# Dealing the last quarter of an MLP output product between the steps of the next product's first quarter

## The chip, the cores and the metric

The kernel runs on one core of one Trainium2 chip. The metric is the device time of one execution in microseconds (us). Most executions of one kernel agree closely. Five engines run side by side, each with its own instruction queue that is worked off in order: TensorE (PE: matrix products, and PEld: its weight loads), VectorE (DVE), ScalarE (ACT), GpSimd (POOL) and SyncE (SP), which here only issues DMA transfers. POOL issues transfers too, the indirect ones (rows picked by an index list) among them.

## The reference, cut to what matters

The reference is one transformer block, forward and backward: `out`, and the gradients of all inputs and weights, for 2048 tokens of width 1024 and an MLP width of 3584, in bf16. The part that counts here is the MLP.

```
x1  = x + ga * fft_filter(LN(x)*(1+ca)+sa)          # earlier in the kernel
n3  = LN(LN(x1)*(1+cb)+sb)
z   = n3 @ w1 + b1 ;  h = gelu(z)                   # "z" blocks
out = x1 + gb * (h @ w2 + b2)                       # output product, "bo"
gz  = (grad_out*gb) @ w2.T * gelu'(z)               # kept in HBM as d_gz
gn3 = gz @ w1.T                                     # input-gradient product, "pg"
... layer-norm backward of gn3, column sums, then the weight gradients
```

## The kernel before, in words

The tokens are cut into four quarters (blocks b = 0 to 3) of 512. The output product of a quarter (`bo_pass`, L802) runs in two passes, h = 0 and 1, one for each half of the width. A pass has seven steps; a step loads 512 KB of `w2` (L812) and issues 16 matmuls of 128x512 into four PSUM banks (L817). Before the first step, four small matmuls put the bias into the banks (L808). After the seventh, ScalarE copies the banks into the tile `otile` (L826), VectorE makes three products and sums of it (L173, the helper `tt`), and the result goes to `out_0` in three transfers: a direct one issued by SP (L155) and then two indirect ones issued by POOL (L160), which in the program wait one for the other. One late part, four matmuls `pa` (L836), sums the columns of a product for the gradient of `gb`; it is taken up a little later by the generator's second `next`.

A list, `plan`, written out by hand, sets the order of z blocks and output steps. In the last quarter (b = 3) no z block is left, so its 14 output steps follow each other. I call them B1 to B14 (B1 to B7 are h = 0, B8 to B14 are h = 1). `ordered()` chains each matmul of these parts behind the last, so TensorE keeps the written order; all other instructions are placed by a scheduler, which also sets the order in the DMA queues.

Then comes the input-gradient product. It needs `w1` transposed: seven tiles `w1T` are loaded with transposing transfers (L949), into buffers that the z blocks' `w1` tiles leave. For each quarter, seven 512 KB tiles of `gz` are loaded (L989, tiles `gzr` in the buffers t0 to t3), and two passes of seven steps of 16 matmuls fill four PSUM banks each (L996). I call the 14 steps of the first quarter G1 to G14. ScalarE copies the banks out with row sums (L1001, tiles `gn3a` and `gn3b` by turns). VectorE then works through a layer-norm backward (L895 to L900, the tile `got` takes its products), a product `pru`, a second layer-norm backward (L1017 and L895 to L900), and `au`. TensorE sums the columns of `gn3`, `pru` and `au` into `acc3a` and `acc3b` (L193), in 24 matmuls a quarter, placed among the next quarter's `pg` matmuls. `got` lies in the buffer that `otile` had, so nothing is written there before the last transfer out of `otile` has landed. Beside this chain, `gmod_ring` (L916 on) makes eight steps for row 5 of the `w_mod` gradient (L934, L936, tiles `gmw` and `gmg`), which need the finished column sum of `gb`, that is the last `pa`, through `d_gmod` in HBM.

Of the kernel before, what the change touches and what calls it, by code (L numbers as in the profile page):

```python
# [10 lines left out]
FP32 = mybir.dt.float32  # L11
BF16 = mybir.dt.bfloat16
I32 = mybir.dt.int32
ACT = mybir.ActivationFunctionType
# [3 lines left out]
P = 128  # L18
S = 2048
D = 1024  # L20
# [4 lines left out]
KH = D // 2  # L25
# [5 lines left out]
NB = 4  # L31
BW = S // NB
# [3 lines left out]
def kernel(  # L36
# [24 lines left out]
    nc = tc.nc  # L61
# [3 lines left out]
    small = ctx.enter_context(tc.tile_pool(name="small", bufs=2))  # L65
    reg = ctx.enter_context(tc.tile_pool(name="reg", bufs=1))
# [4 lines left out]
    W1T = PXT[2:6] + ["sma", "smb", "px0"]  # L71
# [7 lines left out]
    def ps_f(name):  # L79
        return psum.tile([P, 512], FP32, tag="f", name=name, bufs=4)  # L80
# [37 lines left out]
    d_gz_v = d_gz.rearrange("(fc p) s -> p fc s", p=P)  # L118

    def chunk_rows(dt, i):  # L120
        return dt[4 * i * P:4 * (i + 1) * P, :].rearrange("(q p) d -> p q d", p=P)
# [47 lines left out]
    def bcn(row, n):  # L169
        return bass.AP(tensor=row.tensor, offset=row.offset, ap=[row.ap[0], [0, n], row.ap[1]])  # L170

    def tt(out, a, b, op):
        return nc.vector.tensor_tensor(out=out, in0=a, in1=b, op=op)  # L173
# [101 lines left out]
    wt = reg.tile([P, 2, NDC, 256], BF16, name="wt", tag="wt")  # L275
# [44 lines left out]
    for j in range(4):  # L320
        for cch in range(NDC):
# [7 lines left out]
            else:  # L329
                with tc.high_priority():  # L330
                    nc.scalar.activation(out=gBoT[j][:, cch, :], in_=pt[:], func=ACT.Identity, scale=gb_col[:, cch:cch + 1],
                                         accum_out=gu[:, j, cch:cch + 1])
# [315 lines left out]
    last_pe = [None]  # L648

    def ordered():  # L650
        return tc.issue_after(last_pe[0].ins)
# [77 lines left out]
    for g in range(7):  # L729
        wtile = reg.tile([P, NDC, BW], BF16, name=f"w1_{g}", tag=W1T[g])  # L730
# [71 lines left out]

    def bo_pass(b, h):
        cs_ = slice(h * KH, (h + 1) * KH)
        pbs = [(ps_f if b < NB - 1 or h == 0 else (ps_s, ps_d)[k % 2])("pbo") for k in range(4)]
        for i in range(4):
            with ordered():
                last_pe[0] = nc.tensor.matmul(pbs[i][:], lhsT=ones_bf[0:1, :], rhs=b2_row[0:1, cs_], start=True, stop=False)  # L808
        for g in range(7):
            wp = w2p[w2n[0] % 4]  # L810
            w2n[0] += 1
            nc.sync.dma_start(out=wp, in_=w2_v[:, g * 4:(g + 1) * 4, cs_])  # L812
            hh = hh_slots[(b * 7 + g) % 11]
            for i in range(4):
                for k in range(4):
                    with ordered():
                        last_pe[0] = nc.tensor.matmul(pbs[i][:], lhsT=hh[:, k, i * P:(i + 1) * P], rhs=wp[:, k, :],  # L817
                                                      start=False, stop=(g == 6 and k == 3))
            if g < 6:
                yield  # L820
        bo, x1t, go = (otile[0][:, k] for k in range(3))
        nc.sync.dma_start(out=x1t, in_=chunk_rows(d_x1, b)[:, :, cs_])
        load_tok_half(go, grad_out, b, h)
        for i in range(4):
            with tc.high_priority():
                last_ev[0] = nc.scalar.copy(out=bo[:, i, :], in_=pbs[i][:])  # L826
        tt(go, go, bo, ALU.mult)
        tt(bo, bo, bcn(gb_row[:, cs_], 4), ALU.mult)
        tt(bo, bo, x1t, ALU.add)
        store_tok_half(out_0, bo, b, h)  # L830

        yield
        pa = (ps_d if b < NB - 1 else ps_f)("pa")
        for i in range(4):
            with ordered():
                last_pe[0] = nc.tensor.matmul(pa[:], lhsT=ones_bf[:], rhs=go[:, i, :], start=(i == 0), stop=(i == 3))  # L836
        with tc.high_priority():
            if b == 0:
                nc.vector.tensor_copy(out=gacc[:, cs_], in_=pa[0:1, :])  # L839
            else:  # L840
                tt(gacc[:, cs_], gacc[:, cs_], pa[0:1, :], ALU.add)

    def bo_both(b):
        for h in range(2):
            late = bo_pass(b, h)
            for _ in range(7):
                next(late)
                yield
            bo_late.append(late)

    bo_late = []
# [2 lines left out]
    Z_AT = [{1: ((0, 4),), 2: ((0, 5),), 3: ((0, 6),), 4: ((1, 0),), 6: ((1, 1),), 7: ((1, 2),), 9: ((1, 3),), 10: ((1, 4),),  # L854
             11: ((1, 5),), 12: ((1, 6),)}]
    Z_AT += [{k: ((b, g),) for g, k in enumerate((0, 2, 4, 7, 9, 11, 12))} for b in (2, 3)] + [{}]
    for b in range(NB):
        for k in range(14):
            plan += [("z",) + bg for bg in Z_AT[b].get(k, ())] + [("b", b, k)]
    boq = {}  # L860
    for kind, b, g in plan:
# [7 lines left out]
        else:  # L869
# [6 lines left out]
                bo_late.clear()  # L876
            if g == 13:
                next(boq[b], None)
    for late in bo_late:
        next(late, None)  # L880
    store_gmod([gacc[:, 0:KH], gacc[:, KH:D]], 5)

    gb1 = small.tile([P, NFC], FP32, tag="gb1", bufs=1)
# [57 lines left out]
                load_w(n + 2)  # L941
            yield

    w1Ts = []
    for g in range(7):
        wtile = reg.tile([P, 4, D], BF16, name=f"w1T_{g}", tag=W1T[g])
        for k in range(4):
            fc = g * 4 + k
            nc.sync.dma_start_transpose(out=wtile[:, k, :], in_=B_w1[:, fc * P:(fc + 1) * P])  # L949
        w1Ts.append(wtile)  # L950
    gzr = [reg.tile([P, 2, 4, BW], BF16, name=f"gzr{k}", tag=f"t{k}") for k in range(4)]
    gn3s = [reg.tile([P, 4, D], BF16, name="gn3a", tag="uv0"), reg.tile([P, 4, D], BF16, name="gn3b", tag="wt")]
    n3u = reg.tile([P, 4, D], BF16, name="n3u", tag="uv1")
    n2u = reg.tile([P, 4, D], BF16, name="n2u", tag="uv2")
    pru = reg.tile([P, 4, D], BF16, name="pru", tag="uv3")[:]
    got = reg.tile([P, 6, D], BF16, name="got", tag="ot")
    fbuf2 = reg.tile([P, 4, 4, D], BF16, name="fbuf2", tag="fr")
    acc3 = [ps_d("acc3a"), ps_d("acc3b")]
    gzn = 0
    gmw = reg.tile([P, 2, D], BF16, name="gmw", tag="ph")  # L960
    gmg = reg.tile([P, 2, D], BF16, name="gmg", tag="sb")
    early = gmod_ring((5,), [gmw[:, 0], gmw[:, 1], gmg[:, 0]], gmg[:, 1, :])
# [13 lines left out]

    for b in range(NB):
        gn3 = gn3s[b % 2]
        sums = small.tile([P, 2, 4], FP32, tag="sums")
        gzt = []  # L980
        nc.sync.dma_start(out=n3u[:], in_=chunk_rows(d_n3, b))
        nc.sync.dma_start(out=n2u[:], in_=chunk_rows(d_x1, b))
        norm_act(n2u, n2u, 1, b)
        go4 = got[:, 0:4, :]
        load_tok(go4, grad_out, b)
        for g in range(7):
            sl = gzr[gzn % 8 // 2][:, gzn % 2]
            gzn += 1
            nc.sync.dma_start(out=sl, in_=d_gz_v[:, g * 4:(g + 1) * 4, b * BW:(b + 1) * BW])  # L989
            gzt.append(sl)  # L990
        for h in range(2):
            pgs = [ps_f("pg") for _ in range(4)]
            for g in range(7):
                for i in range(4):
                    for k in range(4):
                        nc.tensor.matmul(pgs[i][:], lhsT=gzt[g][:, k, i * P:(i + 1) * P],  # L996
                                         rhs=w1Ts[g][:, k, h * KH:(h + 1) * KH],
                                         start=(g == 0 and k == 0), stop=(g == 6 and k == 3))
            for i in range(4):
                with tc.high_priority():  # L1000
                    nc.scalar.activation(out=gn3[:, i, h * KH:(h + 1) * KH], in_=pgs[i][:], func=ACT.Identity,  # L1001
                                         accum_out=sums[:, h, i:i + 1])
        tt(sums[:, 0, :], sums[:, 0, :], sums[:, 1, :], ALU.add)
        for i in range(4):
            t = 4 * b + i
            ln_bwd(gn3[:, i, :], sums[:, 0, i:i + 1], n3u[:, i, :], stats[:, 2, 0, t:t + 1], gn3[:, i, :], got[:, 4 + i % 2, :])
        next(early, None)
        tt(pru, gn3[:], n2u[:], ALU.mult)
        g2, ftmp = gn3, pru
        if b < NB - 1:  # L1010
            sums3(b, gn3, pru)
        else:
            g2, ftmp = gn3s[0], gzr[0].rearrange("p a b (c d) -> p (a b c d)", c=1).rearrange("p (q d) -> p q d", d=D)
        s2c = small.tile([P, 4], FP32, tag="s2c")
        for i in range(4):
            t = 4 * b + i
            nc.vector.tensor_tensor_reduce(out=g2[:, i, :], in0=gn3[:, i, :], in1=opcb_row, scale=1.0, scalar=0.0,  # L1017
                                           op0=ALU.mult, op1=ALU.add, accum_out=s2c[:, i:i + 1])
            ln_bwd(g2[:, i, :], s2c[:, i:i + 1], n2u[:, i, :], stats[:, 1, 0, t:t + 1], g2[:, i, :], got[:, 4 + i % 2, :])
        next(early, None)  # L1020
        tt(g2[:], g2[:], go4, ALU.add)
        nc.gpsimd.dma_start(out=chunk_rows(d_gx1, b), in_=g2[:])
        nc.sync.dma_start(out=au[:], in_=chunk_rows(d_A, b))
        tt(n3u[:], g2[:], bcn(ga_row, 4), ALU.mult)
        fold_tok(n3u, ftmp)
        fold2_in[b] = fold_d(fbuf2[:, b], n3u[:], ftmp)
        tt(au[:], g2[:], au[:], ALU.mult)
        if b < NB - 1:
            sums3_ga(b, au)
            next(early, None)  # L1030
# [226 lines left out]
```

## Time and profile before

| what | us |
|---|---|
| median of 3 runs | 1522.13 |
| the runs | 1520.72, 1522.13, 1531.21 |
| span of the profiled execution, first to last instruction (the page gives no other time of its own for it) | 1521.4 |
| TensorE busy | 1437.8 |
| VectorE busy | 1072.0 |
| ScalarE busy | 722.1 |
| last quarter of the output product on TensorE | 715.9 to 773.9 |
| first quarter of the input-gradient product starts | 779.8 |
| last matmul of the input-gradient product starts | 996.6 |

All times of single instructions below are counted from the start of the span. In a row of the timeline the first number is the start, the second the busy time of the merged row (so several instructions, where the row ends in x16), then engine, line, operation, tile written <- tiles read; in brackets stands how long the engine was idle before it and what ended that idle time.

### The profile page before, as it was taken

To read this page: it belongs to the slowest core of one execution; us is meant where nothing else is said; L and a number is where in the kernel's file an instruction comes from. 1 tells how busy PE (TensorE), PEld (TensorE's weight loads), DVE (VectorE), ACT (ScalarE), POOL (GpSimd) and SP (SyncE) were. 2 spreads that over 40 slices of the span, in tenths; PEclk is the share of its full clock that TensorE was granted. 3 is DMA by queue.
4 is the path that set the end of the run, shared out by engine and by line. 5 is a ranking of instruction groups with operands and counts; after the bars stand their busy time and mean duration, and the time that the engine had idled before them with its cause. 6 is when DMAs were issued, how large, how long until landed. Compare 5 with 4: busy or idle time off the path is not lost.

```text
span 1521.4 us, 18355 instructions
## 1 busy us (share of the span) xinstructions
PE 1437.8 (95%) x6831; PEld 667.6 (44%) x6831; DVE 1072.0 (70%) x1577; ACT 722.1 (47%) x956; POOL 363.5 (24%) x428
## 2 busy tenths in 40 slices
PE   5889899999999999999989999979998899999998
PEld 2434445444444444444334444434444444444443
DVE  5992868897799887877224977967066666898633
ACT  4765556668876666655012333322522344443211
POOL 5720621111112122220210101311033421322423
PEclk8999999999999999999999999989999999999999
DMA  9972745989587876999956336496288986766996
GB/s 327 282 207 66 198 150 176 280 258 339 193 265 238 211 254 216 257 282 271 322 170 205 135 101 221 109 275 176 63 201 225 235 242 183 197 174 163 257 206 195
DMA packets 358160, 324.27 MB, mean 213 GB/s; under 512 B 209187, under 2 KB 300849, under 8 KB 357816
## 3 DMA queue, kind: packets, MB, share of 16 engines
q1 hardware_dynamic: 324184, 207.71, 52.4%
q0 software_dynamic: 33888, 115.41, 22.5%
q8 instruction: 53, 0.87, 0.2%
q14 instruction: 35, 0.29, 0.1%
HBM read 164.15 MB, written 109.10 MB: 180 GB/s over the span
## 4 chain that ended last, share of the span: by engine, by line
PE 47%; DVE 22%; DMA 10%; issue 10%; ACT 6%; POOL 3%; SPq 1%; POOLq 0%; ACTq 0%; DVEq 0%
PE pbo L817 11%; PE pz L776 9%; PE gw2acc L1090 8%; PE pg L996 5%; DVE ct L173 4%; PE pv L544 3%; PE pu L451 3%; PE gw1acc L1157 2%; PE pp L659 2%; DVE got L895 2%; DVE fbuf L173 1%; DMA gB<-in_grad_out_dram 1%; DVE gn3a L900 1%; DMA out_dram<-otl 1%; DVE gt L173 1%
## 5 line engine op out<-in xcount | busy, mean ns | idle before, releaser
L659 PE MATMUL pp<-gBoT,wt 128*128 128x512 bf16 x896 | 200.4, 379 | 1.9 <-ACT pho L669 1.0
L1157 PE MATMUL gw1acc<-gzh,n3n 128*128 128x512 bf16 x896 | 197.0, 380 | 0.3 <-DMA gzh<-d_gz 0.3
L996 PE MATMUL pg<-w1T,gzr 128*128 128x512 bf16 x896 | 196.3, 380 | 0.4
L776 PEld LDWEIGHTS <-w 128*128 128x128 bf16 x896 | 87.7, 98 | 109.0 <-issue 3.8
L996 PEld LDWEIGHTS <-gzr 128*128 128x128 bf16 x896 | 88.0, 98 | 107.5 <-issue 2.9
L1157 PEld LDWEIGHTS <-n3n 128*128 128x128 bf16 x896 | 87.8, 98 | 104.3 <-issue 0.6
L659 PEld LDWEIGHTS <-wt 128*128 128x128 bf16 x896 | 87.4, 98 | 103.0 <-DMA wt<-in_B_w_dram 1.4
L776 PE MATMUL pz<-n3Tb,w 128*128 128x512 bf16 x448 | 99.1, 379 | 1.5 <-DVE w2sD L839 1.5
L1090 PE MATMUL gw2acc<-gB,hhsA 128*128 128x512 bf16 x448 | 100.1, 379 | 0.0
L776 PE MATMUL pz<-n3Ta,w 128*128 128x512 bf16 x448 | 98.7, 379 | 1.3 <-ACT gt L779 1.3
L817 PEld LDWEIGHTS <-hhA 128*128 128x128 bf16 x608 | 59.9, 99 | 79.0 <-issue 10.8
L1095 ACT CAST gwo<-gw2acc 128x512 bf16<-128x512 f32 x54 | 30.6, 584 | 122.4 <-PE gw2acc L1090 80.1
L779 ACT ACTIVATE gt<-pz,b_col 128x512 bf16<-128x512 f32 x112 | 72.9, 684 | 29.5 <-PE pz L776 29.0
L785 ACT ACTIVATE gt<-gt 128x2048 bf16<-128x2048 bf16 x28 | 53.4, 1910 | 64.4 <-DVE gt L173 64.4
L173 DVE TENSOR_TENSOR gt<-gt,gt 128x2048 bf16<-128x2048 bf16 x56 | 68.5, 1224 | 15.9 <-ACT gt L787 15.1
L1161 ACT CAST gwo<-gw1acc 128x512 bf16<-128x512 f32 x48 | 27.7, 584 | 109.1 <-PE gw1acc L1157 87.5
L173 DVE TENSOR_TENSOR ct<-ct 128x2048 bf16<-128x2048 bf16 x64 | 76.0, 1219 | 0.8
L1090 PE MATMUL gw2acc<-gB,hht 128*128 128x512 bf16 x256 | 58.9, 392 | 8.7 <-DVE gB L173 8.4
L1090 PEld LDWEIGHTS <-hhsA 128*128 128x128 bf16 x448 | 43.8, 98 | 50.4
L781 ACT ACTIVATE gt<-gt 128x2048 bf16<-128x2048 bf16 x28 | 53.5, 1910 | 7.6 <-DVE gb_acc L796 6.9
L787 ACT ACTIVATE gt<-gt 128x2048 bf16<-128x2048 bf16 x28 | 53.3, 1909 | 0.4
L1162 POOL DMA_DIRECT2D out_dram<-gwo x56 | 30.7, 551 | 77.9 <-ACT gwo L1161 38.3
(314 smaller groups left out, 2552.9 us busy)
## 6 DMA issues: line engine op xcount, KB each, us to landing
gzr<-d_gz SPq DMA_DIRECT2D x28, 512.0 KB, 7.7
wblk<-in_w_mod_dram SPq DMA_DIRECT2D x12, 1024.0 KB, 13.4
d_ph<-pho POOLq DMA_DIRECT2D x21, 512.0 KB, 5.2
out_dram<-otl POOLq DMA_DIRECT2D x40, 256.0 KB, 3.7
d_hh<-hhA POOLq DMA_DIRECT2D x19, 512.0 KB, 4.8
w2sD<-in_B_w_dram SPq DMA_DIRECT2D x14, 512.0 KB, 6.1
hhC<-d_ph SPq DMA_DIRECT2D x14, 512.0 KB, 5.1
w2sA<-d_ph SPq DMA_DIRECT2D x14, 512.0 KB, 4.0
```

What stands on the lines that cost most here:

```text
L173: return nc.vector.tensor_tensor(out=out, in0=a, in1=b, op=op)
L451: last_pu[0] = nc.tensor.matmul(pu[:], lhsT=fb[:, i, cl, c8 * P:(c8 + 1) * P], rhs=sm[:, i, :], start=(i == 0), stop=(i == 3))
L659: last_pe[0] = nc.tensor.matmul(pp[:], lhsT=wt[:, fg % 2, cch, k * P:(k + 1) * P], rhs=gBoT[j][:, cch, :], start=(cch == 0), stop=(cch == ...
L776: last_pe[0] = nc.tensor.matmul(pz[:], lhsT=w1s[g][:, cch, k * P:(k + 1) * P], rhs=n3T[:, cch, :], start=(cch == 0), stop=(cch == NDC - 1))
L779: nc.scalar.activation(out=zb[:, k, :], in_=pz[:], func=ACT.Identity, bias=b1_col[:, fc:fc + 1], scale=1.0)
L781: nc.scalar.activation(out=av, in_=zb, func=ACT.Square)
L785: nc.scalar.activation(out=sg, in_=bv, func=ACT.Sigmoid, scale=2.0 * GK)
L787: nc.scalar.activation(out=bv, in_=bv, func=ACT.Sigmoid, scale=-2.0 * GK)
L817: last_pe[0] = nc.tensor.matmul(pbs[i][:], lhsT=hh[:, k, i * P:(i + 1) * P], rhs=wp[:, k, :], start=False, stop=(g == 6 and k == 3))
L996: nc.tensor.matmul(pgs[i][:], lhsT=gzt[g][:, k, i * P:(i + 1) * P], rhs=w1Ts[g][:, k, h * KH:(h + 1) * KH], start=(g == 0 and k == 0), sto ...
L1090: nc.tensor.matmul(acc[:], lhsT=hh_s[hh_o[fc]][:, t, :], rhs=gBs[t // 4][:, t % 4, h * KH:(h + 1) * KH], start=(t == 0), stop=(t == NT - 1))
L1157: nc.tensor.matmul(acc[:], lhsT=n3ns[t // 4][:, t % 4, cch * P:(cch + 1) * P], rhs=gz2[t // 8][:, t % 8, :], start=(t == 0), stop=(t == NT ...
```

## The change

The last quarter leaves `plan`. Its 14 steps are dealt out with the 14 steps of the first input-gradient quarter by a string, in which B is a step of the output product, G one of the input-gradient product and L takes up the late column sums. The `pg` loop becomes a generator `pg_pass`, used with `ordered()` for the first quarter. The `w1T` and `gz` tiles 0 to 2 are asked for ahead of the string, tiles 3 to 6 one by one in the first G steps. The second pass of the last quarter now uses the same four PSUM banks as the first (tag f), the first input-gradient quarter the four banks of tags s and d, and the column sum of the pass B1 to B7 a bank of tag d. `gn3a` moves to the buffer uv3 and `pru` to uv0.

```
-        pbs = [(ps_f if b < NB - 1 or h == 0 else (ps_s, ps_d)[k % 2])("pbo") for k in range(4)]
+        pbs = [ps_f("pbo") for _ in range(4)]
...
-        pa = (ps_d if b < NB - 1 else ps_f)("pa")
+        pa = (ps_d if b < NB - 1 or h == 0 else ps_f)("pa")
...
-    for b in range(NB):
+    for b in range(NB - 1):
         for k in range(14):
             plan += [("z",) + bg for bg in Z_AT[b].get(k, ())] + [("b", b, k)]
...
+    gn3s = [reg.tile([P, 4, D], BF16, name="gn3a", tag="uv3")]
...
+    def pg_pass(b, h, pool):
+        gn3 = gn3s[b % 2]
+        pgs = [pool(k)("pg") for k in range(4)]
+        for g in range(7):
+            for i in range(4):
+                for k in range(4):
+                    with ordered() if b == 0 else ExitStack():
+                        mm = nc.tensor.matmul(pgs[i][:], lhsT=gzs[b, g][:, k, i * P:(i + 1) * P],
+                                              rhs=w1Ts[g][:, k, h * KH:(h + 1) * KH],
+                                              start=(g == 0 and k == 0), stop=(g == 6 and k == 3))
+                    if b == 0:
+                        last_pe[0] = mm
+            if g < 6:
+                yield
+        for i in range(4):
+            with tc.high_priority():
+                nc.scalar.activation(out=gn3[:, i, h * KH:(h + 1) * KH], in_=pgs[i][:], func=ACT.Identity,
+                                     accum_out=g_sums[b][:, h, i:i + 1])
+        yield
+
+    def pg_first():
+        g_sums[0] = small.tile([P, 2, 4], FP32, name="sums", tag="sums")
+        for h in range(2):
+            for g, _ in enumerate(pg_pass(0, h, lambda k: (ps_s, ps_d)[k // 2])):
+                if h == 0 and g + 3 < 7:
+                    load_w1T(g + 3)
+                    load_gz(0, g + 3)
+                yield
+
+    for g in range(3):
+        load_w1T(g)
+        load_gz(0, g)
+    last_bo, pg0 = bo_both(NB - 1), pg_first()
...
+    for step in "BBLBGBGBGBGBGBGBGLBGBGBGBGBGGGL":
+        if step == "L":
+            run_late()
+        else:
+            next(last_bo if step == "B" else pg0)
+    next(last_bo, None)
+    run_late()
     store_gmod([gacc[:, 0:KH], gacc[:, KH:D]], 5)
...
-    pru = reg.tile([P, 4, D], BF16, name="pru", tag="uv3")[:]
+    pru = reg.tile([P, 4, D], BF16, name="pru", tag="uv0")[:]
```

So TensorE's order becomes B1 B2 (late sum of b = 2) B3 G1 B4 G2 B5 G3 B6 G4 B7 G5 B8 G6 B9 G7 (late sum of B1 to B7) B10 G8 B11 G9 B12 G10 B13 G11 B14 G12 G13 G14 (late sum of B8 to B14), and then the second quarter of `pg`.

More of the change, by code (lines that the diff above doesn't have):

```diff
@@ L878, with load_w1T @@
                 next(boq[b], None)
-    for late in bo_late:
-        next(late, None)
+    w1Ts = []
+    gzr = [reg.tile([P, 2, 4, BW], BF16, name=f"gzr{k}", tag=f"t{k}") for k in range(4)]
+    gzs = {}
+    gn3s = [reg.tile([P, 4, D], BF16, name="gn3a", tag="uv3")]
+    g_sums = {}
+    def load_w1T(g):
+        wtile = reg.tile([P, 4, D], BF16, name=f"w1T_{g}", tag=W1T[g])
+        for k in range(4):
+            fc = g * 4 + k
+            nc.sync.dma_start_transpose(out=wtile[:, k, :], in_=B_w1[:, fc * P:(fc + 1) * P])
+        w1Ts.append(wtile)
@@ new lines, in load_gz @@
+    def load_gz(b, g):
+        n = b * 7 + g
+        gzs[b, g] = gzr[n % 8 // 2][:, n % 2]
+        nc.sync.dma_start(out=gzs[b, g], in_=d_gz_v[:, g * 4:(g + 1) * 4, b * BW:(b + 1) * BW])
+    def pg_pass(b, h, pool):
[3 more added lines that the diff above has]
+            for i in range(4):
+                for k in range(4):
+                    with ordered() if b == 0 else ExitStack():
[11 more added lines that the diff above has]
+        yield
@@ new lines, in pg_first, with run_late @@
+    def pg_first():
[10 more added lines that the diff above has]
+    last_bo, pg0 = bo_both(NB - 1), pg_first()
+    def run_late():
+        for late in bo_late:
+            next(late, None)
+        bo_late.clear()
@@ L942, in gmod_ring @@
             yield
[L944 to L952, printed above, removed]
+    gn3s.append(reg.tile([P, 4, D], BF16, name="gn3b", tag="wt"))
     n3u = reg.tile([P, 4, D], BF16, name="n3u", tag="uv1")
     n2u = reg.tile([P, 4, D], BF16, name="n2u", tag="uv2")
-    pru = reg.tile([P, 4, D], BF16, name="pru", tag="uv3")[:]
+    pru = reg.tile([P, 4, D], BF16, name="pru", tag="uv0")[:]
     got = reg.tile([P, 6, D], BF16, name="got", tag="ot")
@@ L958 @@
     acc3 = [ps_d("acc3a"), ps_d("acc3b")]
-    gzn = 0
     gmw = reg.tile([P, 2, D], BF16, name="gmw", tag="ph")
@@ L978 @@
         gn3 = gn3s[b % 2]
-        sums = small.tile([P, 2, 4], FP32, tag="sums")
-        gzt = []
+        if b > 0:
+            g_sums[b] = small.tile([P, 2, 4], FP32, name="sums", tag="sums")
+        sums = g_sums[b]
         nc.sync.dma_start(out=n3u[:], in_=chunk_rows(d_n3, b))
@@ L985 @@
         load_tok(go4, grad_out, b)
[L986 to L992, printed above, removed]
-            for g in range(7):
[L994 to L1002, printed above, removed]
+        if b > 0:
+            for g in range(7):
+                load_gz(b, g)
+            for h in range(2):
+                for _ in pg_pass(b, h, lambda k: ps_f):
+                    pass
         tt(sums[:, 0, :], sums[:, 0, :], sums[:, 1, :], ALU.add)
```

## The prediction

> **What bounds the kernel now.** I read the page first, then TensorE's timeline around the place of the change, then what the waits there hang on, queue by queue.
>
> The page: TensorE is busy for 95% of the span. Only its gaps, and times when it is slow, can be won.
>
> ```profile
> PE 1437.8 (95%) x6831; PEld 667.6 (44%) x6831; DVE 1072.0 (70%) x1577; ACT 722.1 (47%) x956; POOL 363.5 (24%) x428
> ```
>
> TensorE's timeline, from B1 to the first column sums:
>
> ```profile
> 715.11 0.86 PE L808 MATMUL pbo<-b_row,ones_bf 1*128 1x512 bf16 x2 [1.86 <-ACT otile L826]
> 715.90 5.31 PE L817 MATMUL pbo<-w2sD,hhA 128*128 128x512 bf16 x16
> 721.05 3.62 PE L817 MATMUL pbo<-w2sB,hhB 128*128 128x512 bf16 x16
> ...
> 733.23 3.61 PE L817 MATMUL pbo<-w2sD,hhA 128*128 128x512 bf16 x16 [0.67 <-DMA w2sD<-in_B_w_dram]
> ...
> 740.69 3.61 PE L817 MATMUL pbo<-w2sA,hhA 128*128 128x512 bf16 x16 [0.40 <-DMA w2sA<-in_B_w_dram]
> ...
> 747.19 5.30 PE L817 MATMUL pbo<-w2sC,hhA 128*128 128x512 bf16 x16 [1.92 <-DMA w2sC<-in_B_w_dram]
> ...
> 774.32 0.23 PE L188 MATMUL ptr<-fin,gb_bf 128*28 128x128 bf16 x1 [0.24 <-ACT otile L826]
> 778.16 1.86 PE L836 MATMUL pa<-otile,ones_bf 128*128 128x512 bf16 x4 [3.62 <-DVE otile L173]
> 779.83 53.01 PE L996 MATMUL pg<-w1T,gzr 128*128 128x512 bf16 x241
> ```
>
> Two things are to be seen. After B2 the waits are 0.67, 0.40, 1.92, 0.24 and 3.62 us, 6.85 in all. And sixteen matmuls take 3.62 us (3.45 from one group's start to the next, 0.2157 a matmul), but 5.31 and 5.30 right after waits of 1.86 and 1.92 us: a restart costs 1.68 us. After 0.67 it costs nothing. After 3.62 us the late sum takes 1.86 instead of 1.03, and the 241 matmuls 53.01 instead of 52.16 (241 x 0.2157, and 0.16 for the end of the last one): 1.68 again.
>
> Why the `w2` loads are late: the share of the DMA engines in the stretches.
>
> ```profile
> 735.00:748.00 13.00, 10.68 (x48) 4.52 (x47) 0.00 (x0) 1.97 (x4) 3.49 (x4) 0.98 1.08 366
> 800.00:830.00 30.00, 30.00 (x141) 13.61 (x139) 10.65 (x22) 5.50 (x16) 2.69 (x5) 1.00 0.70 227
> ```
>
> The last two columns are DMA share and GB/s: saturated at 735 to 748, not at 800 to 830.
>
> Last, what follows the late output. SP's and POOL's timelines show the store of the last half quarter and the first transfer into its buffer, VectorE's the chain that writes there too:
>
> ```profile
> 725.92 1.28 SPq L155 DMA_DIRECT2D out_dram<-otile  x1
> ...
> 781.95 0.40 SPq L155 DMA_DIRECT2D out_dram<-otile  x1
> ...
> 794.30 0.38 SPq L128 DMA_DIRECT2D got<-in_grad_out_dram  x1
> ```
>
> ```profile
> 785.13 1.00 POOL L160 DMA_INDIRECT out_dram<-otile,xu  x1 [17.33 <-DMA out_dram<-otile]
> 791.15 1.53 POOL L160 DMA_INDIRECT out_dram<-otile,xu  x1 [5.02 <-DMA out_dram<-otile,xu]
> ```
>
> ```profile
> 827.33 1.23 DVE L895 CUSTOM_DVE_ANT_0 got<-gn3a,n3u 128x1024 bf16<-128x1024 bf16 x1 [11.76 <-ACT gn3a L1001]
> ```
>
> From the store's issue to the moment `got` may be written: 794.30 - 781.95 = 12.35 us. Now this is hidden, because VectorE's first write to `got` comes at 827.33. In the changed program that instruction still waits for the same three transfers.
>
> **The change, part by part.** All sums are against the profiled execution (span 1521.4). The median of the runs lies 0.7 above that span, so I add the difference to the median, 1522.1.
>
> *Dealing B and G out.* B3 starts at 725.49, as before: TensorE's order up to there is unchanged. From B3 to B14 lie 12 B and 11 G steps, 368 matmuls, 79.4 us; with the bias (0.86) and a late sum (0.86) B14 ends at 806.6. The `w2` loads have 6.9 us a step instead of 3.45, so the waits of 0.67, 0.40 and 1.92 go, with one restart. The last late sum has G12 to G14 (10.35 us) ahead of it, more than the 5.5 us that ScalarE and VectorE need before it: the 3.62, the 0.24 and the second restart go. Saved: 6.85 + 2 x 1.68 = 10.2.
>
> *Banks.* B8's bias must wait for the copies out of B7's banks; G5 (3.45 us) lies between, and the last copy takes 0.59: nothing; without that cover 1.9, as at 715.11. The late sum behind G7 takes a bank that `pg` has just filled: its copy out is 0.8 us long and starts 0.9 before G7's end, so about 0.4 (bounds 0 and 1.86, that first row). B14 ends at 807.0, G14 at 817.4, the late sum at 818.2, and the second quarter starts at 818.5. Before, the first quarter's 224 matmuls ended at 779.83 + 0.85 + 48.3 = 829.0. TensorE is 10.5 ahead here.
>
> *Loads.* The transposes stand at the same places in SP's queue as before but for the last two (2 x 2.1 us), which go behind the `w2` loads of B3 and B4. Four `gz` loads instead of one go ahead of those. Two transposes less, 3 x 512 KB more at 366 GB/s (4.3 us): the sum is about nothing for B3's load; bounds: nothing, and 4.3 plus a restart, 6.0. Near nothing, since the later `w2` loads gain room. `n3u` and `n2u` go in at about 786, 30 us before use; `gz` tiles of the second quarter follow G8 to G14. Moving `gn3a` and `pru` costs nothing: both buffers are left by then.
>
> *The output's tail, now on VectorE's path.* B14 ends at 807.0, its last copy at 807.8, three VectorE operations of 1.23 later SP stores, at 811.7. With the 12.35 us of the rows above, `got` is free at 824.0. Until then the waiting VectorE instruction holds the whole layer-norm chain of the first quarter behind it, although `gn3a` is there from 818. The other end is the loaded case: from the store at 725.92 to ScalarE's next write into that buffer, at 747.20, it took 21.3 us. I take 12.35, since the DMA engines are not saturated in this stretch.
>
> *The chain after it, by its offsets before.* From the first write to `got` the trace has 5.7 us to the first column sum of `gn3` (833.03), 15.4 to `pru` (842.76) and 39.0 to `au` (866.37).
> - TensorE does 29 `pg` matmuls (6.3 us) and stands at 824.8; the sum is ready at 829.7: a new wait of 4.9 with a restart of 1.68. Two sums and 42 matmuls: 840.9; `pru` is there (839.5). 14 sums, 101 matmuls: 865.7.
> - Row 5 of the `w_mod` gradient, now at 789 to 816 in idle VectorE time, needs the last late sum and moves into this chain: eight steps of 1.15 and 0.44, 12.7 us. Four fall before `au`, 6.4 us, of which some 3 fill the chain's own pauses (1.12, 1.07 and 1.37 before the L900 rows): `au` at 824.0 + 42.5 = 866.5, wait 0.8, sums done at 868.2.
> - Fold work (9.6) and three more such steps (4.8) follow: VectorE starts the second quarter at 881.0 instead of 883.26, although TensorE has finished it at 879.5.
> - TensorE: 78 matmuls to 885.0, wait to 886.7; 40 and `pru` at 896.5, sums to 899.5; 91 to 919.1, `au` at 920.5, done at 922.2. Before that was 924.03, with 11 matmuls less done (605 and 594 by the program order): 1.8 + 2.4 = 4.2 ahead. The third quarter's chain then starts at TensorE's pace, 4.1 ahead, and the rest of the program is ordered as before.
>
> Sum: 10.5 ahead at 818.5; 4.9 + 1.7 and smaller waits lost; 4.1 left. 1522.1 - 4.1 = 1518.0.
>
> [...] The rows show a slow restart after waits of 1.86 and 1.92 us. [...] The granted clock of 0.83 in the stretch 712 to 722, with that 1.86 in it, speaks for the rows. [...]
>
> **The rivals.**
> - *The tail stays hidden.* If the stores land by 819 (7 us), the 4.9 and the restart vanish and all 10.5 stay: 1511.6. For it: the issue-to-landing median of `otile` transfers is 4.6. Against: POOL's two indirect stores follow each other 6.02 us apart. Chance 0.17.
> - *Slower: the tail is as slow as under load.* With 21.3 us `got` is free at 833.0; the whole chain of the first two quarters shifts by 9.0, and 4.2 ahead become 4.8 behind: 1526.9. It decides from 16.5 us on. For it: the three `gz` loads of 512 KB close by. Against: 0.70 DMA share at 800 to 830. Chance 0.15.
> - *The `w2` load of B3 is late* behind four `gz` loads: up to 6.0, 1524.0. Chance 0.08.
> - *Half of the change does not take place*: the transposes keep their places. True by the program order, and without a price.
>
> **How the numbers follow.** The forecast, 1518.0, has 0.55, with an own range of 1514 to 1522 (the tail between 10 and 16 us). The range 1510 to 1528 takes in the rivals at 1511.6, 1524.0 and 1526.9 and leaves out 0.05 of unforeseen cases. A measurement of this kernel tells about 1% (15.2 us) from no change. No case reaches that: even all of the 10.2 us is too little for faster, and slower needs a tail of 33 us or waits that I have not seen. From the unforeseen cases: faster by over 1% 0.05, within 0.89, slower 0.06.
>
> **What would show it.** In the changed profile: no DMA wait before a `pbo` row after B3; the last L836 row without idle time; the first `pg` matmul of the second quarter near 818.5; the first VectorE row that writes `got` near 824, its idle time ended by an `out` transfer and not by `gn3a`; a TensorE wait of some 5 us before the first L193 row; `gmw` rows among those of the first quarter's chain; the last `pg` matmul near 992.5. Wrong would be the forecast if `got` starts before 820 or after 828, if B3 to B7 wait for DMA, or if TensorE makes good the wait of 4.9 later.

## The result and the profile after

The changed kernel takes 1532.03 us (median of 18 runs, 1527.93 to 1539.23); the kernel before, on the same chips, 1525.2 us (median of 18, 1517.02 to 1533.04). The ratio is 1.0053, with a 95% interval from 1.0038 to 1.0068: some 8 us slower (1525.2 x 0.0053 = 8.1), where 4.1 us less was forecast. The profiled execution of the changed kernel has a span of 1537.1 us and a time of its own of 1539.23, the longest of its 18, so some of its waits can be longer than usual; the experiments show that the one before B3 is.

First the page's line of busy times. TensorE's work is the same (some of its records are missing here, 6697 of 6831), and VectorE's too. What has grown is the time between.

```profile
PE 1430.7 (93%) x6697; PEld 668.2 (43%) x6831; DVE 1070.9 (70%) x1577; ACT 722.8 (47%) x956; POOL 367.1 (24%) x428
```

TensorE's timeline of the changed kernel, from B1 to the second quarter's first column sums:

```profile
718.10 5.31 PE L817 MATMUL pbo<-w2sD,hhA 128*128 128x512 bf16 x16
...
734.69 6.01 PE L817 MATMUL pbo<-w2sA,hhB 128*128 128x512 bf16 x16 [6.96 <-DMA w2sA<-in_B_w_dram]
...
828.88 1.03 PE L836 MATMUL pa<-otile,ones_bf 128*128 128x512 bf16 x4
...
838.35 0.38 PE L193 MATMUL acc3a<-gn3a,sel 128*128 128x512 bf16 x1 [1.92 <-DVE gn3a L962]
...
849.74 0.38 PE L193 MATMUL acc3a<-pru,sel 128*128 128x512 bf16 x1 [1.73 <-DVE pru L173]
...
875.91 0.38 PE L193 MATMUL acc3a<-au,sel 128*128 128x512 bf16 x1 [1.19 <-DVE au L173]
...
903.68 0.59 PE L193 MATMUL acc3a<-gn3b,sel 128*128 128x512 bf16 x1 [9.05 <-DVE gn3b L962]
...
904.48 9.96 PE L904 MATMUL pg<-w1T,gzr 128*128 128x512 bf16 x39
```

Two waits stand out. Before B3, 6.96 us for its `w2` load, and B3 then takes 6.01 instead of 3.62 us: 9.4 in all. Before the first column sum of the second quarter, 9.05 us for `gn3b`, and from that sum to the first one of `pru` (914.28) it is 10.6 us, where the kernel before needs 9.2 (888.91 to 898.64, without its wait of 0.50): 1.4 more. Between the two everything is as it was meant: no wait for DMA after B3, and the last late sum (828.88) without idle time.

In the balance of the two profiled executions B1 starts 2.2 us later (718.10 against 715.90, in work that the change does not touch); the second quarter then starts at 830.0, and the last `pg` matmul of all quarters ends at 1010.7 instead of 997.0; what is left takes 526.4 instead of 524.4. So of 15.7 us, 2.2 lie ahead of the change, 11.5 in it and 2.0 behind it.

What SP's queue did in the two places, from its timeline (start, time in the queue's issuing, and what was issued):

```profile
712.91 6.84 SPq L889 DMA_TRANSPOSE w1T<-in_B_w_dram  x2
719.86 4.28 SPq L895 DMA_DIRECT2D gzr<-d_gz  x4
724.23 2.73 SPq L812 DMA_DIRECT2D w2sA<-in_B_w_dram  x1
...
823.21 0.39 SPq L155 DMA_DIRECT2D out_dram<-otile  x1
...
850.17 15.20 SPq L985 DMA_DIRECT2D gmw<-in_w_mod_dram  x2
...
888.38 0.34 SPq L985 DMA_DIRECT2D gmw<-in_w_mod_dram  x1
...
889.96 0.63 SPq L1035 DMA_DIRECT2D n3u<-d_n  x1
```

B3's load is issued at 724.23 and lands at 734.69, 10.4 us later. In the second place two reloads of `gmw` take 15.20 us, and the load of `n3u` goes out at 889.96, right after a third. The table of SP's waits says why (us in total, times, longest):

```profile
SPq L985 <- DMA out_dram<-gmw: 37.4, 3, 14.5
```

A reload of `gmw` waits until the store out of it has landed, 14.5 us in the longest case, and everything behind it in SP's queue waits too: the `gz` load behind the two reloads goes out at 865.46, when their 15.20 us are over. The store itself is late, for POOL issues it behind the indirect loads of `got`; POOL's timeline:

```profile
872.68 7.46 POOL L131 DMA_INDIRECT got<-in_grad_out_dram,xu  x1 [0.30 <-issue]
880.44 1.97 POOL L131 DMA_INDIRECT got<-in_grad_out_dram,xu  x1 [0.30 <-issue]
882.41 1.16 POOL L999 DMA_DIRECT2D out_dram<-gmw  x2
```

VectorE's timeline shows the chain that hangs on it:

```profile
833.07 1.23 DVE L957 CUSTOM_DVE_ANT_0 got<-gn3a,n3u 128x1024 bf16<-128x1024 bf16 x1 [1.75 <-issue]
...
881.85 2.35 DVE L173 TENSOR_TENSOR pru<-n3u 128x2048 bf16<-128x2048 bf16 x2
...
898.22 1.22 DVE L957 CUSTOM_DVE_ANT_0 got<-gn3b,n3u 128x1024 bf16<-128x1024 bf16 x1 [4.97 <-DMA n3u<-d_n]
```

`n3u` is read for the last time until 884.2 (881.85 + 2.35), its next load is issued 5.8 us after that, and lands 8.1 us after its issue; only then can VectorE start the second quarter. In the kernel before, SP's and VectorE's rows of the same two moments are these; the load has the time in which VectorE waits for `gn3b`:

```profile
873.41 0.37 SPq L981 DMA_DIRECT2D n3u<-d_n  x1
```

```profile
883.26 1.22 DVE L895 CUSTOM_DVE_ANT_0 got<-gn3b,n3u 128x1024 bf16<-128x1024 bf16 x1 [7.49 <-ACT gn3b L1001]
```

### The profile page after: what moved, and what is told of

It reads as the page before. It is cut to its first block, busy times and chain, and to the rows that moved or that the text cites. A ratio compares the mean times of both kernels' runs of the same rounds, so it can differ in the third digit from the quotient of the medians.

```text
span 1537.1 us, 18218 instructions
## 1 busy us (share of the span) xinstructions
PE 1430.7 (93%) x6697; PEld 668.2 (43%) x6831; DVE 1070.9 (70%) x1577; ACT 722.8 (47%) x956; POOL 367.1 (24%) x428
## 4 chain that ended last, share of the span: by engine, by line
PE 51%; DVE 19%; DMA 11%; issue 10%; ACT 5%; POOL 3%; SPq 1%; POOLq 0%; DVEq 0%; ACTq 0%
PE pbo L817 11%; PE pz L776 9%; PE gw2acc L1133 9%; PE pg L904 5%; PE gw1acc L1200 4%; PE pv L544 3%; DVE ct L173 3%; PE pu L451 3%; PE pp L659 2%; DVE fbuf L173 1%; DVE got L957 1%; DMA out_dram<-otl 1%; DMA gB<-in_grad_out_dram 1%; PE po L609 1%; DVE x L173 1%
## 5 line engine op out<-in xcount | busy, mean ns | idle before, releaser
L173 DVE TENSOR_TENSOR otile<-otile 128x2048 bf16<-128x2048 bf16 x16 | 19.5, 1220 | 70.2 <-ACT otile L826 70.1
```

## The experiments

Two theories stood against each other. Q: the loss lies in the order of SP's queue, ahead of B3 and ahead of the second quarter's `n3u`, with the eight row-5 steps in VectorE's chain beside it. S: the DMA engines are too busy, so a wait that is taken away comes back elsewhere. Medians of different jobs differ by a few us for one and the same kernel (the kernel before had 1523.19 to 1526.26), so I compare ratios to the kernel before, each from its own job (6 to 12 runs of a kernel, 29 to 34 of the kernel before); 0.001 is 1.5 us. A gain on the changed kernel is the difference of two such ratios, and the two intervals together are some 0.0025 to 0.0035 wide to each side: a gain under some 4 us is not clear of noise.

**e1: the first `gz` loads behind B3's `w2` load.**

```
+            w2_in[0] = nc.sync.dma_start(out=wp, in_=w2_v[:, g * 4:(g + 1) * 4, cs_])
...
+        with tc.issue_after(w2_in[0].ins) if b == 0 else ExitStack():
+            nc.sync.dma_start(out=gzs[b, g], ...)
...
         load_w1T(g)
-        load_gz(0, g)
...
+    for n, step in enumerate("BBLBGBGBGBGBGBGBGLBGBGBGBGBGGGL"):
+        if n == 4:
+            for g in range(3):
+                load_gz(0, g)
```

> The changed kernel, with the gz loads of the first quarter put behind the w2 load of the latest B step in SP's queue; all else as in the changed kernel. Theory Q (order in SP's queue): the wait of 6.96 us before B3 and its slow restart (2.4) are there because four gz loads stand ahead of B3's w2 load. Then that wait falls under 1 us, G1 waits no longer than 2 us for its gz tile, and the kernel gains 6 to 9 us on the changed one (ratio to before 0.998 to 1.002). Theory S (the DMA engines are saturated, the order only chooses who waits): the wait moves to G1 or to B4, the sum of the TensorE waits between B2 and G3 stays over 5 us, and the gain is under 3 us.

Measured: 1530.56 us, ratio 1.0032 (1.0013 to 1.0050), 3.2 us less than the change (0.0021 x 1525): half of the least that Q expected, just above what S did (under 3), and not clear of noise. In its profile there is no wait before B3; the rest is as it was:

```profile
828.91 0.38 PE L193 MATMUL acc3a<-gn3a,sel 128*128 128x512 bf16 x1 [2.01 <-DVE gn3a L966]
...
894.69 0.59 PE L193 MATMUL acc3a<-gn3b,sel 128*128 128x512 bf16 x1 [8.76 <-DVE gn3b L966]
```

The wait before B3 is not always 9.4 us long. Seven of the profiled kernels have the four `gz` loads ahead of B3's load: the wait was 6.96, 3.11, 0, 2.54, 0, 3.34 and 3.27 us (changed, e2, e4, e5, e6, e7, e11), with slow matmuls behind three of them (2.4, 1.7, 1.7): 3.6 us in the mean. The five with the `gz` loads behind it (e1, e8, e9, e10, e12) show none. But this does not show that the `gz` loads are the cause, for the twelve differ in something else. Some 25 us ahead of B3's load, at a place where all kernels have the same order, SP cannot load `hhC` again before a store of `gz` out of that buffer has landed. SP's waits, in the changed kernel and in the one before:

```profile
SPq L770 <- DMA d_gz<-hhC: 5.6, 1, 5.6
SPq L770 <- DMA d_gz<-hhC: 0.2, 1, 0.2
```

For this load the hold-up was 5.0 to 5.9 us in four of the profiles with a wait before B3 (changed, e2, e7, e11) and 0.2 at most in all others with the change's order; the fifth, e5, has none, but TensorE came to B3 1.7 us earlier there, since its B1 did not run slow. None of the five with the `gz` loads behind B3's load had the hold-up, so they can't show that their order takes the wait away. What the `gz` loads ahead do show: where TensorE waited for B3's load, it began 10.4 to 11.3 us after that load's issue; in the order of before it was 7.3 us at most, and 6.7 in e3.

**e2: no row-5 steps, and e3: the kernel before without them.** In both the generator `early` is replaced by an empty one, so both leave out row 5 of the `w_mod` gradient.

```
-    early = gmod_ring((5,), [gmw[:, 0], gmw[:, 1], gmg[:, 0]], gmg[:, 1, :])
-    next(early)
+    early = iter(())
```

> The changed kernel without the eight steps of row 5 of the w_mod gradient (this row of the output is left out, and its part of the gradient of c). Theory Q: the wait of 9.05 us in front of the first column sum of the second quarter comes from n3u, whose load stands in SP's queue behind reloads of gmw; without the steps it falls to 1 us or less, and VectorE starts the second quarter's chain 8 us or more earlier against TensorE. Gain on the changed kernel 5 to 9 us. The rival, that the waits there come from the late got buffer alone, expects no gain above 2 us.

> The kernel before without the same eight steps (the same row left out). They lay there in VectorE's idle time and their loads behind the n3u load. Theory Q and its rivals expect no gain: within 1.5 us of the kernel before. If it gains 4 us or more, what the changed kernel gains without the steps is no cost of the change.

Measured: e2 1519.5 us, ratio 0.9967 (0.9937 to 0.9996), 13 us less than the change, more than the 5 to 9 expected; e3 1526.18 us, ratio 0.9997 (0.9978 to 1.0016). Before the change the steps cost nothing that the interval (some 3 us) can tell; in the changed order taking them out wins all that was lost, or more. In e2's profile the wait for `gn3b` is 1.25 us (the profiled execution, 1529.05 us, is one of its two longest, so its span is no measure of the gain). The surprise was in e3, where nothing of the dealing is in the program:

```profile
734.97 5.18 PE L818 MATMUL pbo<-w2sA,hhB 128*128 128x512 bf16 x16 [7.57 <-DMA w2sA<-in_B_w_dram]
```

So B3's load can be late in the order of before as well; it was in one of its two profiles, behind the longest hold-up of `hhC` of all, 9.7 us. How much of B3's wait is a cost of the change stays open.

**e4: eight buffers in place of the ring of three.** No reload has to wait for a store.

```
-    early = gmod_ring((5,), [gmw[:, 0], gmw[:, 1], gmg[:, 0]], gmg[:, 1, :])
+    early = gmod_ring((5,), [fbuf2[:, 2 + k // 4, k % 4] for k in range(8)], gmg[:, 1, :])
...
-            nc.sync.dma_start(out=bufs[n % 3], in_=w_mod[...])
+            nc.sync.dma_start(out=bufs[n % len(bufs)], in_=w_mod[...])
```

> The changed kernel with eight buffers for the steps of row 5 (in a tile that is still unused there) instead of a ring of three, so that no load waits for a store; the same work on VectorE. Theory Q: the n3u load of the second quarter is no longer held up, its chain starts when VectorE is free (some 5 us earlier than in the changed kernel, against the start of G14), the wait of 9.05 falls to 3 to 5 us, and the gain is 3 to 6 us. The rival that the 12.7 us of VectorE work are the cost expects a gain under 2 us here and 5 or more without the steps.

Measured: 1526.33 us, ratio 1.0005 (0.9985 to 1.0025), 7.3 us less than the change, although the steps are still done in the chain. The load of `n3u` goes out when its buffer is left (876.78), and the wait for `gn3b` is 4.96 us, as expected. But `got` is written first 13.4 us after the store's issue (813.59 to 827.02) instead of 9.9, and TensorE waits 5.5 us for `gn3a`. The eight loads stand around that store in SP's queue; that they are the reason is not shown.

**e5: the dealing undone, the rest of the change kept.**

```
-    for step in "BBLBGBGBGBGBGBGBGLBGBGBGBGBGGGL":
+    for step in "BBLBBBBBBBLBBBBBGGLGGGGGGGGGGGG":
```

> Only the order of the steps is changed: B3 to B14 follow each other again, the last late sum comes after G2, and G3 to G14 follow; transposes, loads, buffers and the rest of the change stay. Theory Q (the loss lies in SP's queue, ahead of B3 and at the second quarter's n3u, and the dealing itself wins what was forecast): the waits for w2 between B4 and B14 come back with a restart (0.67 + 0.40 + 1.92 + 1.68, 4.7 us), the wait of VectorE for got's buffer goes (1.9 us on TensorE), the hold-up of n3u stays, since the row-5 steps keep their place in SP's queue behind the gz loads: 1533 to 1537 us against some 1526 before. Rival S (the dealing itself costs, by the load that it puts on the DMA engines): 1526 or less, as before.

Measured: 1532.05 us, ratio 1.0039 (1.0015 to 1.0063), not distinguishable from the change. S expected 1526 or less and falls here. Q misses its range by 1 us: the waits for `w2` did not come back in this profile (there is one before B3, 2.54 us, and one for banks before B8's bias, 2.39 with a restart), so the loads had found their room without the dealing. In the profiles the dealing still wins 4.6 us of its stretch: from B2 to the end of the late sum it is 101.7 us here without B3's wait, against 97.1 dealt, in e9 (counted from B2, since B1 ran slow in e9 alone). The time does not show it; the hold-up of `n3u`, which comes behind, is there as in the changed kernel: 9.36 us for `gn3b`.

**e6: the load of `n3u` ahead of three reloads.** Only the order in SP's queue differs from the changed kernel.

```
-            nc.sync.dma_start(out=bufs[n % 3], in_=w_mod[...])
+            with tc.issue_after(n3_in[0].ins) if r == 5 and n >= 5 else ExitStack():
+                nc.sync.dma_start(out=bufs[n % 3], in_=w_mod[...])
...
-        nc.sync.dma_start(out=n3u[:], in_=chunk_rows(d_n3, b))
+        n3_in[0] = nc.sync.dma_start(out=n3u[:], in_=chunk_rows(d_n3, b))
```

> The changed kernel, with SP's last three reloads of gmw and gmg placed behind the second quarter's load of n3u, and nothing else. Theory Q: n3u is issued at once when its buffer is left, some 4 to 6 us earlier, the wait of 9.05 us for gn3b before the first column sum of the second quarter falls to 3 to 5 us, and the time to 1526 to 1529 us (4 to 7 less than the change). Rival S (the transfers are slow, whatever their order) and the rival that VectorE's work of the row-5 steps alone makes the chain late: within 2 us of the change, 1531 to 1534.

Measured: 1525.07 us, ratio 1.0011 (0.9984 to 1.0038), 6.4 us less than the change. SP's and TensorE's timelines:

```profile
873.57 0.37 SPq L1037 DMA_DIRECT2D n3u<-d_n  x1
874.03 1.35 SPq L987 DMA_DIRECT2D gmg<-in_w_mod_dram  x1
877.73 1.15 SPq L987 DMA_DIRECT2D gmw<-in_w_mod_dram  x2
```

```profile
888.61 0.59 PE L193 MATMUL acc3a<-gn3b,sel 128*128 128x512 bf16 x1 [5.34 <-DVE gn3b L963]
```

The wait falls from 9.05 to 5.34 us. What is left of it is the load's own time: VectorE starts 9.6 us after the issue. No buffer, no byte and no instruction was taken away, so the queue's order alone carries a large part of the loss (a gain of 6.4 us against a loss of 8.1; the intervals leave the gain between some 2 and 11), as Q said and S did not. For what is left S is not refuted: from 873.6 to 883.1, while this load is on its way with `gz` loads beside it, the DMA share is 1.05 and 389 GB/s are moved.

**e7: the row-5 steps done near the end, ahead of row 2.**

```
+    gmod_row(5, w1g["ins"])
     for r in (2, 1, 0):
```

> The changed kernel, with the eight row-5 steps taken out of the first quarters' chain and done near the end, by the helper that does rows 2, 1 and 0 there; everything is computed. Theory: their 12.7 us on VectorE and their loads in SP's queue are what makes the second quarter's chain late, and VectorE has room at the end (busy 75 of the last 137 us in the changed kernel): 1518 to 1523 us, close to the 1519.5 without the steps. Rival (the work has to be paid wherever it is put): 1527 to 1533.

Measured: 1532.36 us, ratio 1.0034 (1.0007 to 1.0062), far outside the 1518 to 1523 expected. This looked as if the work had to be paid anywhere. But up to its last `pg` matmul (996.2 us) its profile is nearly as good as that of e2 (1.87 us for `gn3b`), and the time behind that point is 537.1 us, where the kernel before has 524.4. The next run shows where.

**e8: `gz` loads as in e1, row 5 as in e7, and only B3 to B9 dealt.**

```
-    for step in "BBLBGBGBGBGBGBGBGLBGBGBGBGBGGGL":
+    for step in "BBLBGBGBGBGBGBGBGLBBBBBGGLGGGGG":
```

> Three edits on the changed kernel: the first gz loads go behind B3's w2 load, the row-5 steps go to the end, and only B3 to B9 are dealt with G1 to G7 while B10 to B14 follow each other, so that the last store out of otile begins some 17 us earlier. Theory Q: no wait before B3, no wait for got's buffer, no hold-up of n3u, up to 2 us of waits for w2 in B10 to B14: 1512 to 1518 us, faster than both kernels. Rival S: the loads of B10 to B14 come late as in the kernel before (some 5 us with a restart): 1519 to 1524.

Measured: 1527.74 us, ratio 1.0018 (0.9990 to 1.0047), outside the ranges of both theories. From B1 to 987 us there is no wait above 1.6 us; most of the gain is lost at one place, as TensorE's and SP's timelines show:

```profile
1464.03 55.95 PE L1201 MATMUL gw1acc<-gzh,n3n 128*128 128x512 bf16 x248 [11.15 <-DMA gzh<-d_gz]
```

```profile
1438.74 10.50 SPq L977 DMA_DIRECT2D wrw<-in_w_mod_dram  x4
1449.33 9.19 SPq L1148 DMA_TRANSPOSE gzh<-d_gz  x1
```

Four loads for such a row hold SP for 10.50 us, since they wait for buffers that VectorE must leave, and the transposing load that TensorE needs stands behind them. It is the same fault in another place; in e7 the same row of TensorE has a wait of 7.30 us.

**e9: the edits of e1 and e6 together, and e10: also no wait for `otile`'s last stores.** The edit that e10 adds:

```
+        lt = fbuf2[:, 1] if b == 0 else got[:, 4:6]
...
-            ln_bwd(..., got[:, 4 + i % 2, :])
+            ln_bwd(..., lt[:, i % 2, :])
```

> The edits of e1 and e6 together: B3's w2 load ahead of the gz loads, the second quarter's n3u ahead of the gmw and gmg reloads; nothing else of the change is touched. Theory Q: the two add up (3.2 and 6.4 us against the change in their own runs), no wait before B3, about 5 us before gn3b: 1520 to 1525 us, a ratio to before of 0.997 to 1.000, what was forecast for the change with some us of the row-5 work on top. Rival S (a wait that is taken away in one place comes back in another): 1526 or more, no better than e6 alone.

> As e9, and the first quarter's layer-norm products go to an unused buffer instead of got, so that VectorE does not wait for the last stores out of otile. If the tail of the output holds the chain as in the prediction's sum, the wait of some 1.9 us for gn3a goes (with a restart of 1.7 where there was one) and the later waits shrink with it: 2 to 5 us less than e9. If the chain is made late by the row-5 steps alone: no difference above 1.5 us to e9.

Measured: e9 1524.05 us, ratio 1.0002 (0.9983 to 1.0022), 7.8 us less than the change; e10 1521.73 us, ratio 0.9988 (0.9972 to 1.0004). e9 is a little better than e6, by less than the intervals can tell, so it is not shown that the two edits add up; its ratio lies just above the 1.000 up to which Q expected it. In e10 TensorE does not wait for `gn3a` at all, but 3.17 us for banks a little later and 5.49 for `gn3b` as in e9. The 2.3 us between the two are what was expected of the tail, but the intervals overlap: how much the tail costs stays open.

**e11: row 5 after row 0, and e12: e8 with row 5 after row 0.**

```
     for r in (2, 1, 0):
         gmod_row(r, w1g["ins"])
         fill(8)
+    gmod_row(5, w1g["ins"])
     fill(NFC * 4 - done[0])
```

> As e7, but row 5 is done after row 0, behind the last loads of the w1 gradient in SP's queue, where e8 showed a wait of 11.15 us of TensorE for such a load behind row 5's reloads. Everything is computed. If that queue was what ate e7's gain: 1519 to 1523 us, near the 1519.5 of the kernel without the steps. If the steps cost their time wherever they stand: 1527 or more.

> As e8, with row 5 after row 0 as in e11: the gz loads behind B3's w2 load, only B3 to B9 dealt with G1 to G7, the row-5 steps at the end. The profile of e8 had 11.15 us of wait and a restart of 1.7 in TensorE's last stretch and no wait over 2 us ahead of it up to 980; without them 1512 to 1517 us, a ratio to before of about 0.993. If other waits follow at the end (VectorE then has 16 such steps in the last 100 us): 1518 to 1524.

Measured: e11 1521.53 us, ratio 0.9989 (0.9972 to 1.0007), against 1.0034 in e7, which differs from it by the place of one line, 6.9 us that the intervals leave clear of noise; e12 1514.75 us, ratio 0.9944 (0.9923 to 0.9964). e12 is the best of all, 8.5 us faster than the kernel before (1523.19 x 0.0056). VectorE's and SP's timelines of e12:

```profile
818.88 1.21 DVE L961 CUSTOM_DVE_ANT_0 got<-gn3a,n3u 128x1024 bf16<-128x1024 bf16 x1
...
873.22 1.23 DVE L961 CUSTOM_DVE_ANT_0 got<-gn3b,n3u 128x1024 bf16<-128x1024 bf16 x1 [6.33 <-DMA n3u<-d_n]
```

```profile
864.51 0.37 SPq L1036 DMA_DIRECT2D n3u<-d_n  x1
```

The chain begins without waiting for `otile`'s stores, `n3u`'s load goes out 45.6 us later, and the second quarter starts 10.0 us ahead of the kernel before (883.26).

The same three moments, read in the same rows of each profile, say in one table where the change lost its lead:

| kernel | VectorE's first write to `got` | load of `n3u` issued | later by | VectorE starts the second quarter | later by |
|---|---|---|---|---|---|
| before | 827.33 | 873.41 | 46.1 | 883.26 | 9.9 (waits for `gn3b`) |
| changed | 833.07 | 889.96 | 56.9 | 898.22 | 8.3 |
| e6, `n3u` first | 821.79 | 873.57 | 51.8 | 883.16 | 9.6 |
| e9, both | 820.04 | 871.80 | 51.8 | 881.47 | 9.7 |
| e2, no row 5 | 827.87 | 873.44 | 45.6 | 881.87 | 8.4 |
| e11, row 5 last | 828.13 | 874.57 | 46.4 | 883.37 | 8.8 |
| e12 | 818.88 | 864.51 | 45.6 | 873.22 | 8.7 |

The row-5 steps in the chain cost 5.7 us (51.8 against 46.1), the held queue another 5.1 (56.9 against 51.8), and the load of 8 to 10 us stands behind both.

## Why the prediction was wrong

- **Dealing: right in its sum.** From B1 to the start of the second quarter were forecast 818.5 - 715.9 = 102.6 us; the changed kernel took 830.0 - 718.1 - 9.4 (B3) = 102.5. After B3 no `w2` load was late, and the late sums cost nothing. The dealing is not the reason for all of it: from B2 to the second quarter's start, without B3's wait, the kernel before needs 107.9 us, e5 101.8 and e9 97.2, so e5 keeps 6 of the 10.7 us without dealing.
- **Banks: right** within what can be seen: no wait there.
- **Loads: mis-sized.** "About nothing" was put for B3's load, with an upper bound of 6.0; the mean over seven profiles is 3.6, the profiled execution has 9.4. Not the issuing failed: from `hhC`'s load to B3's load SP needed 25.2 us (699.07 to 724.23), before 24.9 (693.32 to 718.19). But `hhC`'s load went out 3.5 us later, beyond the 2.2 that the whole execution was late, behind the hold-up of 5.6 us at a place where both programs have the same order; and with four tiles of `gz` just ahead B3's load took 10.4 us to land, where in the kernel before it took 7.3 (B3 starts at 725.49 without a wait). The sum counted their bytes against the transposes' time, not against the load's landing. From the load's issue to B3 the DMA share was 1.23 and 349 GB/s were moved (724.2 to 734.7); in the kernel before it was 1.06 and 343 (718.2 to 725.5). At 349 GB/s the 3 us between 10.4 and 7.3 are some 1 MB, two of the three `gz` tiles that stood ahead in addition: an estimate from these numbers, which no run shows by itself. The rival "the `w2` load of B3 is late", given 0.08, came true in part, by a hold-up that it did not name and, by that estimate, by the `gz` loads that it did.
- **The output's tail: 9.9 us from the store's issue to the first write (823.21 to 833.07), not 12.35.** VectorE's row of that write names no releaser, but SP's load into `got`, which waits for the last store out of `otile`, goes out beside it, at 833.15. The rival of the slow tail (21.3) fell. The wait behind it was 1.92 without a restart, where 4.9 with 1.68 was forecast: 4.7 us better.
- **"VectorE starts the second quarter at 881.0": the step that failed.** It is 57.0 us behind the first write to `got`; measured were 65.2 (833.07 to 898.22). I had let VectorE go on as soon as its fold work was done, and had not asked when `n3u` could be there. Its buffer is left only by the fold work, so its load can't start sooner, and takes 8 to 10 us. In the kernel before the load, issued at 873.41, was covered by the wait for `gn3b` (883.26); I moved TensorE ahead and VectorE's chain back, and so took the cover away without naming it. To that came the 5.8 us in SP's queue. I had listed the row-5 steps as VectorE time only; each of them also issues a load on SP and a store on POOL, and a ring of three buffers ties the one to the other. In the terms of the table: 46.1 + 5.7 + 5.1 + 8.3 = 65.2. With the wait of 9.05 and 1.4 behind it, instead of 1.7, this step costs 8.7 us.
- **The sum.** TensorE's lead of 10.5 was to shrink by 6.3 in the chain; in the profiled execution it shrank by 12.6 (8.7 more for `gn3b`, 4.7 less for the tail, some 2 more for `pru`, `au` and the third quarter's sums). With 9.4 for B3, and 2.2 and 2.0 outside the change: -4.1 + 6.3 + 9.4 + 4.2 = 15.8, measured 15.7. With the mean of 3.6 for B3 and nothing outside: 5.8, beside 5.8 to 10.4 from the ratio's interval; since the kernel before can wait at B3 too, a part of what was measured is not accounted for.
- **The rival "the tail stays hidden", 1511.6,** fits another kernel: e12, which hides it and has the row-5 steps out of the way, gains 8.5 us. How much of that is the tail is not shown.

What stays open: why the store out of `hhC` lands late in some executions and not in others; what B3's wait costs the change against the kernel before; what the tail is worth by itself (e10); and how much of e12's gain needs the dealing.

## What to carry to other kernels

When a chain moves, list for each of its steps the transfers as well as the instructions, and for each transfer three things: when its buffer is left, what stands ahead of it in the issuing queue and may wait, and how long it takes to land; a load that was hidden under a wait is on the path as soon as that wait goes (here `n3u`'s, for which VectorE waited 4.97 us). Small work in an idle stretch (here eight steps of 1.6 us) is sure to be free only there: before it is moved, look at which queue its reloads stand in, and put the load that the critical engine needs ahead of any reload that waits for a store. When a removed piece of work "has to be paid anywhere", look for the place before believing it: moving one line behind the last urgent load took e7 to e11.

## What the runs showed of the hardware

- Slow matmuls behind a wait do not follow from the length of the wait. After 1.85 or 1.86 us before B1's bias the 16 matmuls of B1 took 5.31 us in the changed kernel, e2, e3, e6, e7 and e9 (a restart of 1.69), 6.31 to 6.37 in e1, e4 and e10, and 3.63 (none) in e5, e8, e11 and e12. After 1.92 and 1.73 (`gn3a`, `pru`) there was none; after 2.54 and 3.11 us before B3 (e5, e2) none; after 3.34 and 3.27 (e7, e11) 1.68 each; behind 2.01 us for `gn3a` 1.7 in e11 and none in e1. The granted clock goes with it: from 712 to 722, a stretch with B1's wait in it, it was 0.83 in the kernel before and in e9 and 0.85 in the changed one, where B1 ran slow, and 1.00 in e12, where it did not. What decides between the two is not shown.
- Where VectorE waited for the load of `n3u` (1 MB), it started 8.3 to 10.0 us after the load's issue. The DMA engines were full in that time, with `gz` loads beside it: a share of 1.06 and 368 GB/s in the kernel before (873.4 to 882.0), 0.98 and 343 in the changed one (890.0 to 898.0), 1.07 and 367 in e12 (864.5 to 873.2).
- The two indirect stores of the tail were issued 3.2 us apart in the changed kernel (827.20 and 830.43), 6.0 before.
- Two transposing loads took SP 6.84 us ahead of B3 in the changed kernel; before, four took 8.27 at that place.
